# Moving the second block's sums, one weight conversion and one expert's matrix in an attention, experts and dense kernel

## The chip, the cores and the metric

The kernel runs on one core of a Trainium2 chip. The metric is the device time in microseconds of one execution. An execution is one launch of one program, which holds all three parts of the computation.

A core has five engines that each run their own list of instructions in order and wait for one another by semaphores: TensorE (PE; matrix products, its weight loads shown as PEld), VectorE (DVE), ScalarE (ACT), GpSimd (POOL) and SyncE (SP). Transfers are issued by SyncE and GpSimd here. "Issue" of a transfer and its landing are told apart below.

## The reference, cut to what matters

Three functions are chained. 4 x 8 heads, 1152 positions and a head dimension of 64 give 2304 tokens of 512 after attention.

```python
def attention(q, k, v):
    q_pool = q.reshape(B, H, S // 2, 2, D).mean(axis=3)
    a = softmax(q_pool @ k.T / sqrt(D))
    return a @ v                          # 2304 tokens x 512 in the end

def experts(x, w_skip, w_gate, w1, w2):
    do = x @ w_skip > 0                   # the others pass unchanged
    e = argmax(x[do] @ w_gate); gate = its softmax
    for e in range(8):                    # w1[e] 512x1024, w2[e] 1024x512
        y[mask_e] = gate * (relu(x[mask_e] @ w1[e]) @ w2[e])
    x[do] += y

def dense(x, w_in, w_out):                # w_in 512x2048, w_out 2048x512, both float64
    h = x @ w_in
    return ((h - tanh(h)) @ w_out).astype(float32)
```

The two matrices of the last part come in as float64, 8 MB each. The kernel reads them as pairs of 32-bit words and makes a high and a low part of each on the chip ("conversion" below).

## The kernel before

**Order.** The program is written under a manual schedule: each engine runs its instructions in the order in which the Python code writes them down. So the place of a line in the code is its place in the queue of its engine, and an instruction that waits holds back all that stands behind it on that engine. Attention and the router come first, then `Experts`, then `Dense`.

**Wide: the float64 matrices.** `Wide` cuts both matrices into 16 jobs of 1 MB of raw words, 8 of `w_in` (results in `wi`) and then 8 of `w_out` (results in `wo`). `load(i)` sends job i from SyncE's queue into one of two raw buffers, `raw[i % 2]`. The conversion of a job is three VectorE operations on 128x1024 words (`steps`, lines 769 to 773, into the tile `wa`), then a ScalarE copy for the high part (line 783) and one VectorE operation for the low part (line 784 or 785). `queue` makes a list of small steps of several jobs: the ScalarE copy and the low part of one job are woven into the first steps of the next, and the load of job i + 2 is sent with the third step of job i. So a list of n jobs has 4n pieces, the last of which holds the last copy and low part.

**Experts.** The tokens are sorted by expert on the chip, experts by falling count of tokens, in tiles of 128. How many there are is known only on the chip, so tiles stand in nested conditions that every engine takes with its own branch (`place`, `chain`, `tile`; lines 952, 973 and 977). A tile (`tile(a, j)`: expert a, tile j) gathers its tokens, multiplies by the first matrix (line 917, `ps_bh`), by the second (line 917 too, `ps_by`), and stores the result to DRAM (`ys`) in the next tile. `load(a, i)` sends the first (i = 0, buffers `f1`) or second (i = 1, buffers `f2`) matrix of expert a from GpSimd's queue, in two halves of 1 MB, behind a condition on the count of tokens; the count `n` and the expert's number `e` are read into registers of GpSimd with the first matrix. `split1` and `split2` turn pieces of the matrices into a high and a low float16 part (`c1`, `c2`; named `w1s`, `w2s` in the trace) with one ScalarE and one VectorE operation each, line 877 and the line behind it. The first matrix of expert a + 1 is sent in the first tile of expert a, once the last `split1` of a is written down; its second matrix later in the same tile. Three `split1` pieces of the next expert stand at the end of an expert's last tile, behind a condition. `SIDE` says how many jobs of `Wide` are converted in which tile (11 in all; `Dense.LATE` must hold the rest), and the loads for the next tile's jobs stand at the end of each tile.

**The way to the dense stage.** `Experts.run` stores the last tile from GpSimd; `before` sends the gather for block 0 of the dense stage from GpSimd; `after` (`Dense.first`) takes the very last tile's rows from SBUF by a product with a selection matrix.

**Dense.** The 2304 tokens are 9 blocks of 256. `fetch(n)` loads a block's rows from SyncE (`fetch_x`) and gathers the experts' results by two gathers on GpSimd (`fetch_y`, tile `cy`, line 1054). `mix(n, a)` adds gate times expert result to half a block on VectorE (line 1064). `transp(n, a)` makes a high part on ScalarE (line 1092) and a low part on VectorE (line 1093), and sends two transposing transfers from SyncE (line 1096) into `xT`; block 0 is transposed on TensorE instead. A step `(n, u)` is an eighth of the hidden dimension for a block: `hid` makes 24 matrix products (lines 1108 to 1110), three ScalarE operations, five VectorE operations (lines 1119 to 1123), a ScalarE copy (1124) and a subtraction on GpSimd (1125). `proj` takes the results of the step two before and makes 12 products with `w_out` (lines 1141 to 1143). The first 16 steps go over blocks 0 and 1 in the order four steps of block 0, four of block 1, then alternating; steps 16 to 71 take blocks 2 to 8 one after the other. So step 4 is the first that needs block 1.

Beside the steps, `run` takes one piece of the list of late conversions in each step (two in steps listed in `TWICE`), and by `side` the sums and transposes of blocks 1 and 2: halves of block 1 behind steps 1 and 2, of block 2 behind steps 9 and 11. `setup` sends the first two raw loads of the late jobs before anything else of this stage, and `fetch(1)` stands in `run`.

Of the kernel before, what the change touches and what calls it, by code (L numbers as in the profile page):

```python
# [9 lines left out]
F32 = mybir.dt.float32  # L10
# [470 lines left out]
E = 8  # L481
# [328 lines left out]
class Experts:  # L810
# [6 lines left out]
    SX, S1, S2 = 2.0 ** 8, 2.0 ** 4, 2.0 ** 8  # L817
    SIDE = {(0, 1): 2, (0, 2): 2, (0, 3): 2, (0, 4): 1, (1, 1): 2, (1, 2): 1, (1, 3): 1}

# [33 lines left out]
    def load(self, a, i, half=(0, 1)):  # L853

        if a == E:
            return
        nc, pool = self.nc, (mybir.EngineType.Pool,)
        if i == 0 and 0 in half:
            self.n, self.e = self.reg(self.perm[:, 0], a, self.MOST[a], pool), self.reg(self.perm[:, 1], a, E - 1, pool)
        with self.tc.If(self.n > 0) if a else ExitStack():  # L860
            src = (self.w1, self.w2)[i][ds(self.e, 1)].rearrange("o (k p) f -> p (o k) f", p=P)
            for k in half:
                nc.gpsimd.dma_start(out=(self.f1, self.f2)[i][k],
                                    in_=src[:, 4 * k:4 * k + 4] if i else src[:, :, 512 * k:512 * k + 512])
# [14 lines left out]

    def split1(self, f):  # L880
        w = slice(f * P, (f + 1) * P)
        v = slice(f % 4 * P, (f % 4 + 1) * P)
        self.split([t[:, :, w] for t in self.c1], self.f1[f // 4][:, :, v], self.S1)

# [22 lines left out]
    def tile(self, a, j, base, n):  # L907
# [11 lines left out]
        if j == 0:  # L919
            for f in range(self.PRE, 8):  # L920
                self.split1(f)
            self.load(a + 1, 0)
        aside(3)
# [27 lines left out]
        if a + 1 < E:  # L951
            with self.tc.If(self.end <= j + 1):
                for f in range(self.PRE):
                    self.split1(f)
        aside(len(side))
        if a + j:
            for i in self.groups.get((a, j + 1), ())[:2]:
                self.wide.load(i)

    def place(self, a):  # L960
# [20 lines left out]
    def run(self, before, after):  # L981
        nc = self.nc
        self.fetch(0)
        self.load(0, 0, (1,))
        self.load(0, 1)
        last = self.reg(self.more[:, 0], 0, CAP - 1, (mybir.EngineType.Pool,))
        nc.scalar.activation(self.py.rearrange("p (a t) -> p a t", a=4),
                             self.ident32.unsqueeze(1).to_broadcast([P, 4, P]), AF.Copy, scale=0.0)
        T = mybir.EngineType
        T = (T.Activation, T.Pool, T.DVE, T.SP)  # L990
        self.tiles = self.count(0)
        for f in range(2):
            self.split1(f)
        self.transp()
        for f in range(2, self.PRE):
            self.split1(f)
        self.fetch(1)
        few = self.reg(self.more[:, 0], 1, 1, T)
        self.place(0)
        self.tc.mark_branch_hint_location("few", hint=few, engines=T)  # L1000
        before()
        self.evac()
        self.store(last)
        after()
        with self.tc.If(few > 0, label="few"):
            some = [self.reg(self.perm[:, 0], a, self.MOST[a], T) for a in range(2)]
            for (a, j), jobs in self.groups.items():
                with self.tc.If(some[a] <= j):
                    for i in jobs:
                        self.wide.load(i)  # L1010
                        self.wide.run([i])


class Dense:


    T2 = 0.04
    LATE = 5
    TWICE = (5, 6, 7, 8)
    ORDER = (0, 8, 1, 2, 3, 4, 5, 6, 7)  # L1020
# [7 lines left out]

    def setup(self, ctx, wide):
        tc, self.wide = self.tc, wide  # L1030
        jobs = range(len(wide.jobs) - self.LATE, len(wide.jobs))
        for i in jobs[:2]:
            wide.load(i)
        self.late = wide.queue(jobs, jobs[2:])
        pool = lambda n, b: ctx.enter_context(tc.tile_pool(name=n, bufs=b))
        self.wp = pool("c_w", 1)
        self.io, self.xt, self.tm, self.gp = pool("c_io", 2), pool("c_xt", 2), pool("c_tm", 2), pool("c_g", 4)
        ps = lambda n, b: ctx.enter_context(tc.tile_pool(name=n, bufs=b, space=PSUM))
        self.ps_h, self.ps_o = ps("ps_ch", 4), ps("ps_co", 4)

# [120 lines left out]
    def run(self):  # L1161
# [7 lines left out]
        NB = NT // 2  # L1169
        self.fetch(1)  # L1170
        for a in range(2):
            self.transp(0, a)
        halves = [(n, u) for u0 in (0, 4) for n in range(2) for u in range(u0, u0 + 4)]
        steps = halves[:8] + sorted(halves[8:], key=lambda s: (s[1], s[0])) + [(n, u) for n in range(2, NB) for u in range(8)]
        side = {1: (1, 0), 2: (1, 1), 9: (2, 0), 11: (2, 1)}
        for s, (n, u) in enumerate(steps):
# [3 lines left out]
            for _ in range(2 if s in self.TWICE else 1):  # L1180
                if self.late:
                    self.late.pop(0)()
            if s in side:
                self.mix(*side[s])
                self.transp(*side[s])
            if n > 1 and u in (2, 4):
# [15 lines left out]
def pooled_attention__moe__tanhshrink_kernel(ctx, tc, q, k, v, moe_w_skip, moe_w_gate, moe_w1, moe_w2,  # L1202
                                             moe2_w_in, moe2_w_out, out):
    nc = tc.nc
# [6 lines left out]
    with tc.manual_schedule():  # L1211
# [59 lines left out]
        with ExitStack() as cctx:  # L1271
            dense.setup(cctx, Wide(cctx, tc, moe2_w_in, moe2_w_out, wi, wo))
            dense.run()
# [30 lines left out]
```

## Time and profile before

| | us |
|---|---|
| Median of three runs | 1036.32 |
| Lowest and highest of them | 1034.73, 1036.73 |
| The profiled execution, its own time | 1031.25 |
| Span of the profiled execution | 1029.8 |
| TensorE busy in it | 937.1 (91%) |
| VectorE busy | 780.3 (76%) |
| ScalarE busy | 633.4 (62%) |
| GpSimd busy | 517.3 (50%) |

TensorE's granted clock is 0.966 of full speed in the mean. The time of a profiled execution and its span differ by what lies before the first and after the last instruction; both are of one execution, and the profiled one lies below the median of the runs. A share of busy time is a mean over three stages that have different limits, so the table says little of what a change in one stage does; the page's strip of 40 slices and the timelines do.

### The profile page before, as it was taken

Reading aid. Unit: us, or ns where it says so; the run is one execution under the profiler, and the core shown is the slowest. Engines: PE = TensorE matmul, PEld = TensorE weight load, DVE = VectorE, ACT = ScalarE, POOL = GpSimd, SP = SyncE. Lnnn points to the kernel's source line nnn. Section 1 sums busy time; section 2 is a strip of 40 time slices with the busy share of each in tenths; the row PEclk is TensorE's granted clock in tenths of the full one; section 3 lists DMA queues with packets and bytes.
Section 4 is the critical chain, followed back from the end, with each engine's and each line's share of the span. In section 5 each row is a group of like instructions: output and inputs, shape, how many; then the busy total and the mean of one; then the engine's idle time right before and its main releaser. Section 6 shows DMA issues by size and latency. Waiting matters only on the chain. (4 is left out here: it accounts for less than half of the span.)

```text
span 1029.8 us, 25570 instructions
## 1 busy us (share of the span) xinstructions
PE 937.1 (91%) x10249; PEld 700.1 (68%) x10249; DVE 780.3 (76%) x1436; ACT 633.4 (62%) x1203; POOL 517.3 (50%) x476
## 2 busy tenths in 40 slices
PE   5689999999999999949999676998999999999998
PEld 2356666666666666637776544876888888888886
DVE  8689889888888998768887547788566566666654
ACT  4588999888999998835353534444445444454443
POOL 7958998888899986533132221323222322322221
PEclk9899999999999999978999888999999999999999
DMA  7776978666785730059774535221221211112100
GB/s 222 152 162 192 207 186 214 135 127 109 168 160 129 156 72 15 28 197 348 231 242 163 191 90 162 71 52 44 60 52 40 64 42 52 52 34 70 21 22 20
DMA packets 129728, 122.43 MB, mean 119 GB/s; under 512 B 92270, under 2 KB 96878, under 8 KB 128558
## 3 DMA queue, kind: packets, MB, share of 16 engines
q1 hardware_dynamic: 121790, 92.48, 36.1%
q0 software_dynamic: 7792, 28.05, 8.2%
q8 instruction: 86, 1.41, 0.6%
q14 instruction: 60, 0.49, 0.2%
HBM read 74.73 MB, written 19.14 MB: 91 GB/s over the span
## 5 line engine op out<-in xcount | busy, mean ns | idle before, releaser
L242 POOL TENSOR_TENSOR pl<-p,ph 128x512 f16<-128x512 f32 x214 | 264.6, 1256 | 55.4 <-ACT p L237 41.5
L188 DVE TENSOR_REDUCE m<-ps_m 128x1 f32<-128x384 f32 x432 | 225.2, 546 | 35.2 <-PE ps_m L187 32.9
L1125 POOL TENSOR_TENSOR gl<-v,gh 128x512 fp32r<-128x512 f32 x71 | 93.6, 1319 | 290.0 <-ACT gh L1124 286.6
L236 ACT ACTIVATE ph<-ps_e 128x512 f16<-128x512 f32 x279 | 176.9, 634 | 53.9 <-PE ps_e L248 50.7
L1108 PE MATMUL ps_ch<-xT,wi 128*128 128x256 f16 x576 | 159.7, 277 | 10.0 <-DMA xT<-xs 9.3
L299 PEld LDWEIGHTS <-ph 128*128 128x128 f16 x2304 | 132.6, 99 | 49.5 <-issue 22.3
L1124 ACT CAST gh<-v 128x512 fp32r<-128x512 f32 x72 | 44.5, 618 | 189.4 <-DVE v L1123 189.4
L1109 PE MATMUL ps_ch<-xT,wi 128*128 128x256 f16 x576 | 158.9, 276 | 0.4 <-DVE xT L1093 0.4
L1110 PE MATMUL ps_ch<-xT,wi 128*128 128x256 f16 x576 | 158.9, 276 | 0.0
L187 PE MATMUL ps_m<-ks,qT 128*128 128x384 f16 (+1 forms) x480 | 121.6, 334 | 23.7 <-DVE m L188 16.3
L299 PE MATMUL ps_a<-vh,pl 128*128 128x65 f16 x1152 | 135.9, 195 | 0.0
L299 PE MATMUL ps_a<-vh,ph 128*128 128x65 f16 x1152 | 135.9, 195 | 0.0
L299 PE MATMUL ps_a<-vl,ph 128*128 128x65 f16 x1152 | 135.7, 194 | 0.0
L237 ACT ACTIVATE p<-ps_e 128x512 f32<-128x512 f32 x211 | 134.5, 637 | 0.0
L1119 DVE SCALAR_TENSOR_TENSOR v<-u,ps_ch 128x512 f32<-128x512 f32 x72 | 49.3, 685 | 111.7 <-ACT t L1117 109.0
L1141 PE MATMUL ps_co<-wo,gh 128*128 128x512 f32 x288 | 120.4, 418 | 3.1 <-ACT wo L783 3.1
L1143 PE MATMUL ps_co<-wo,gl 128*128 128x512 f32 x288 | 114.6, 398 | 0.7 <-POOL gl L1125 0.7
L1142 PE MATMUL ps_co<-wo,gh 128*128 128x512 f32 x288 | 114.2, 397 | 1.0 <-DVE wo L785 1.0
L247 PE MATMUL ps_e<-qT,ks 128*128 128x512 f16 x288 | 110.8, 385 | 2.6 <-DVE pl L242 1.8
L248 PE MATMUL ps_e<-qT,kh 65*128 65x512 f16 x288 | 111.3, 386 | 1.9 <-DMA qT<-mt 1.9
L299 PEld LDWEIGHTS <-pl 128*128 128x128 f16 x1152 | 107.9, 98 | 0.0
L187 PEld LDWEIGHTS <-qT 128*128 128x128 f16 (+1 forms) x480 | 42.7, 101 | 66.0 <-issue 31.3
(222 smaller groups left out, 2084.7 us busy)
## 6 DMA issues: line engine op xcount, KB each, us to landing
v<-in_v_dram SPq DMA_DIRECT2D x16, 576.0 KB
k<-in_k_dram SPq DMA_DIRECT2D x15, 576.0 KB
q<-in_q_dram SPq DMA_DIRECT2D x16, 512.0 KB
raw<-in_moe_w_in_dram SPq DMA_DIRECT2D x8, 1024.0 KB
w1f<-in_moe_w_dram POOLq DMA_DIRECT2D x8, 1024.0 KB, 6.9
w2f<-in_moe_w_dram POOLq DMA_DIRECT2D x8, 1024.0 KB, 9.6
raw<-in_moe_w_out_dram SPq DMA_DIRECT2D x8, 1024.0 KB
ys<-zero SPq DMA_DIRECT2D x5, 1280.0 KB
```

The lines of the kernel that those rows point to most:

```text
L187: nc.tensor.matmul(ps[o, 0:384], w, ks[:, h, c * 384:(c + 1) * 384], start=True, stop=True)
L188: nc.vector.tensor_reduce(out=s["m2"][:, i, c:c + 1], in_=ps[:, 0:384], axis=AX.X, op=ALU.max)
L236: nc.scalar.activation(ph, ps, AF.Exp, scale=2.0 ** -20)
L237: nc.scalar.activation(src, ps, AF.Exp, scale=2.0 ** -20)
L242: (nc.vector if dve else nc.gpsimd).tensor_tensor(out=pl, in0=src, in1=ph, op=ALU.subtract)
L299: self.nc.tensor.matmul(o, x, r, start=first and i == 0, stop=k == NKT - 1 and i == 2, skip_group_check=True)
L1108: nc.tensor.matmul(ps[:, a], self.wi[0][:, w], xh[:, c], start=c == 0, stop=False)
L1109: nc.tensor.matmul(ps[:, a], self.wi[0][:, w], xl[:, c], start=False, stop=False)
L1110: nc.tensor.matmul(ps[:, a], self.wi[1][:, w], xh[:, c], start=False, stop=c == 3)
L1141: nc.tensor.matmul(o, gh[:, a, s], self.wo[0][:, w], start=f == 0, stop=False)
L1142: nc.tensor.matmul(o, gh[:, a, s], self.wo[1][:, w], start=False, stop=False)
L1143: nc.tensor.matmul(o, gl[:, a, s], self.wo[0][:, w], start=False, stop=f == 15)
```

## The change

Three parts, with the lines that carry each.

- **Dense stage.** `side` becomes `{0: ((1, 0), (1, 1)), ...}`: both sums of block 1, then both halves' copies, subtractions and transposes, behind step 0 instead of one half each behind steps 1 and 2. `LATE` is 4 instead of 5 and `TWICE` is (0, 3) instead of (5, 6, 7, 8). `setup` is cut in two: the first sends `fetch(1)`, and `start` behind it the first two raw loads.
- **Experts, conversions.** `SIDE[(1, 2)]` is 2 instead of 1, so that 12 of the 16 jobs are converted beside the experts.
- **Experts, matrices.** The first matrix of expert a + 1 is sent in the first tile of a only for a < 2. For 0 < a < 6 the first matrix of expert a + 2 is sent at the end of the last tile of a, behind a new condition, from GpSimd's queue. For that the first matrices of experts 3, 5 and 7 lie in the two raw buffers of `Wide` (`first`). Where the second matrix is sent for a > 2, the count and the expert's number are read into registers again.

```diff
-    SIDE = {(0, 1): 2, (0, 2): 2, (0, 3): 2, (0, 4): 1, (1, 1): 2, (1, 2): 1, (1, 3): 1}
+    SIDE = {(0, 1): 2, (0, 2): 2, (0, 3): 2, (0, 4): 1, (1, 1): 2, (1, 2): 2, (1, 3): 1}
...
-        if i == 0 and 0 in half:
+        if i == 0 and 0 in half or i and a > 2:
             self.n, self.e = self.reg(self.perm[:, 0], a, ...), self.reg(self.perm[:, 1], a, ...)
         with self.tc.If(self.n > 0) if a else ExitStack():
...
-                nc.gpsimd.dma_start(out=(self.f1, self.f2)[i][k],
+                nc.gpsimd.dma_start(out=(self.first(a), self.f2)[i][k],
...
+    def first(self, a):
+        if a < 3 or a % 2 == 0:
+            return self.f1
+        return [t.rearrange("p (o f) t -> p o (f t)", o=4).bitcast(F32) for t in self.wide.raw]
+
-    def split1(self, f):
+    def split1(self, a, f):
...
         if j == 0:
             for f in range(self.PRE, 8):
-                self.split1(f)
-            self.load(a + 1, 0)
+                self.split1(a, f)
+            if a < 2:
+                self.load(a + 1, 0)
...
         if a + j:
             for i in self.groups.get((a, j + 1), ())[:2]:
                 self.wide.load(i)
+        if 0 < a < E - 2:
+            with self.tc.If(self.end <= j + 1):
+                self.load(a + 2, 0)
...
-    LATE = 5
-    TWICE = (5, 6, 7, 8)
+    LATE = 4
+    TWICE = (0, 3)
...
-    def setup(self, ctx, wide):
+    def setup(self, ctx):
...
+        self.fetch(1)
+
+    def start(self, wide):
         jobs = range(len(wide.jobs) - self.LATE, len(wide.jobs))
         for i in jobs[:2]:
             wide.load(i)
...
-        self.fetch(1)
         for a in range(2):
             self.transp(0, a)
...
-        side = {1: (1, 0), 2: (1, 1), 9: (2, 0), 11: (2, 1)}
+        side = {0: ((1, 0), (1, 1)), 9: ((2, 0),), 11: ((2, 1),)}
...
-            if s in side:
-                self.mix(*side[s])
-                self.transp(*side[s])
+            for f in (self.mix, self.transp):
+                for x in side.get(s, ()):
+                    f(*x)
...
-            dense.setup(cctx, Wide(cctx, tc, moe2_w_in, moe2_w_out, wi, wo))
+            dense.setup(cctx)
+            dense.start(Wide(cctx, tc, moe2_w_in, moe2_w_out, wi, wo))
             dense.run()
```

## Rows read from the trace of the kernel before

**Rows 1.** Table by stretches: stretch, us, busy us of each engine (instructions), clock, DMA.
```profile
core 0: us, PE busy (x) PEld busy (x) DVE busy (x) ACT busy (x) POOL busy (x), PEclk, DMA share, GB/s
650.00:713.00 63.00, 62.67 (x420) 50.83 (x417) 53.89 (x75) 28.55 (x49) 18.24 (x13) 1.00 0.23 59
...
717.80:721.20 3.40, 3.40 (x10) 2.62 (x9) 3.20 (x6) 0.62 (x1) 1.35 (x2) 0.50 0.55 120
```
**Rows 2.** TensorE's timeline, dense stage: start, us, line, operation, [idle before, releaser].
```profile
625.16 0.50 PE L1143 MATMUL ps_co<-wo,gl 128*128 128x512 f32 x1 [0.53 <-POOL gl L1125]
...
627.61 0.28 PE L1108 MATMUL ps_ch<-xT,wi 128*128 128x256 f16 x1
...
642.50 0.37 PE L1108 MATMUL ps_ch<-xT,wi 128*128 128x256 f16 x1 [9.31 <-DMA xT<-xs]
...
649.74 0.28 PE L1108 MATMUL ps_ch<-xT,wi 128*128 128x256 f16 x1
...
710.06 0.28 PE L1108 MATMUL ps_ch<-xT,wi 128*128 128x256 f16 x1
...
715.95 0.50 PE L1141 MATMUL ps_co<-wo,gh 128*128 128x512 f32 x1 [3.10 <-ACT wo L783]
...
721.63 0.28 PE L1108 MATMUL ps_ch<-xT,wi 128*128 128x256 f16 x1
```
**Rows 3.** TensorE's timeline, third expert's tile and fourth's: first-matrix matmuls.
```profile
568.91 5.52 PE L917 MATMUL ps_bh<-bxt,w1s 128*128 128x128 f16 x96 [1.07 <-PEq L973]
...
587.78 7.28 PE L917 MATMUL ps_bh<-bxt,w1s 128*128 128x128 f16 x96 [7.73 <-ACT w1s L877]
```
**Rows 4.** The page's list of DMA issues: count, KB each, us to landing.
```profile
w1f<-in_moe_w_dram POOLq DMA_DIRECT2D x8, 1024.0 KB, 6.9
```
**Rows 5.** VectorE's timeline, dense stage, steps 0 to 2 and a later sum.
```profile
620.06 0.69 DVE L1119 SCALAR_TENSOR_TENSOR v<-u,ps_ch 128x512 f32<-128x512 f32 x1 [6.27 <-ACT t L1117]
...
622.95 0.68 DVE L769 TENSOR_SCALAR wa<-raw 128x1024 uint32<-128x1024 uint32 x1
...
627.66 1.21 DVE L771 SCALAR_TENSOR_TENSOR wa<-raw,wa 128x1024 uint32<-128x1024 uint32 x1
628.79 1.75 DVE L1064 SCALAR_TENSOR_TENSOR cx<-cy,gate,cx 128x512 f32<-128x512 f32 x1
...
694.15 0.74 DVE L1064 SCALAR_TENSOR_TENSOR cx<-cy,gate,cx 128x512 f32<-128x512 f32 x1
```
**Rows 6.** The chain that ended last, just before TensorE's wait at 642.50 ends.
```profile
638.07 0.63 ACT xs L1092
...
638.72 3.65 DMA xT<-xs
```
**Rows 7.** SyncE's timeline: issue times of transposes and of a raw slice.
```profile
631.24 2.59 SPq L1096 DMA_TRANSPOSE xT<-xs  x2
...
636.39 0.38 SPq L762 DMA_DIRECT2D raw<-in_moe_w_out_dram  x1
```
**Rows 8.** GpSimd's timeline, step 1's subtraction.
```profile
628.50 1.50 POOL L1125 TENSOR_TENSOR gl<-v,gh 128x512 fp32r<-128x512 f32 x1 [3.39 <-ACT gh L1124]
```
**Rows 9.** View of tile cy, 614 to 617 us: the gathers for the second block.
```profile
DMA to landing us min/median/max: 8.7/8.7/8.7
```
**Rows 10.** TensorE's branches at the tiles' ends: count: min/median/max ns, starts.
```profile
L973 PEldq COMPARE_BRANCH  x2: 189/271/353, 564.2 to 568.0; - x2
...
L973 PEldq COMPARE_BRANCH  x1: 7422/7422/7422, 579.5 to 579.5; - x1
...
L977 PEldq COMPARE_BRANCH  x2: 185/1948/3710, 599.9 to 604.0; - x2
...
L952 PEldq COMPARE_BRANCH  x2: 72/134/197, 563.8 to 563.9; - x2
```
**Rows 11.** ScalarE's waits, 564 to 570 us: us, count, longest.
```profile
ACT w1s L877 <- issue: 4.2, 1, 4.2
```
**Rows 12.** GpSimd's register loads and semaphore adjustments, 589 to 598 us.
```profile
L846 POOLq TENSOR_LOAD <-perm x4: 287/290/291, 591.2 to 594.6; - x4
...
L860 POOLq INC_SWDGE_SEM  x2: 928/942/957, 592.8 to 596.4; - x2
```

More of the change, by code (lines that the diff above doesn't have):

```diff
@@ L878, in split @@
         self.nc.vector.scalar_tensor_tensor(out=lo, in0=src, scalar=s, in1=hi, op0=ALU.mult, op1=ALU.subtract)
-    def split1(self, f):
+    def first(self, a):
[3 more added lines that the diff above has]
+    def split1(self, a, f):
         w = slice(f * P, (f + 1) * P)
         v = slice(f % 4 * P, (f % 4 + 1) * P)
-        self.split([t[:, :, w] for t in self.c1], self.f1[f // 4][:, :, v], self.S1)
+        self.split([t[:, :, w] for t in self.c1], self.first(a)[f // 4][:, :, v], self.S1)
     def split2(self, f):
@@ L953, in tile @@
                 for f in range(self.PRE):
-                    self.split1(f)
+                    self.split1(a + 1, f)
         aside(len(side))
@@ L992, in run @@
         for f in range(2):
-            self.split1(f)
+            self.split1(0, f)
         self.transp()
         for f in range(2, self.PRE):
-            self.split1(f)
+            self.split1(0, f)
         self.fetch(1)
@@ L1027, in __init__ @@
         self.X[0] = [pool.tile([P, 2, DM], F32, name="c%s0" % n) for n in "xy"]
-    def setup(self, ctx, wide):
-        tc, self.wide = self.tc, wide
+    def setup(self, ctx):
+        pool = lambda n, b: ctx.enter_context(self.tc.tile_pool(name=n, bufs=b))
+        self.wp = pool("c_w", 1)
+        self.io, self.xt, self.tm, self.gp = pool("c_io", 2), pool("c_xt", 2), pool("c_tm", 2), pool("c_g", 4)
+        ps = lambda n, b: ctx.enter_context(self.tc.tile_pool(name=n, bufs=b, space=PSUM))
+        self.ps_h, self.ps_o = ps("ps_ch", 4), ps("ps_co", 4)
+        self.fetch(1)
+    def start(self, wide):
         jobs = range(len(wide.jobs) - self.LATE, len(wide.jobs))
@@ L1034, in setup @@
         self.late = wide.queue(jobs, jobs[2:])
[L1035 to L1039, printed above, removed]
     def fetch(self, n):
```

## The prediction

> **What bounds the kernel now.** I read the page first, for the stages: attention to 440 us, routing, the experts to 601, a handover, and the dense stage from 613 to the end. The diff touches nothing before the experts, so the question is who ends the waits from 465 us on. The table by stretches answers it for most of the dense stage: from 650 to 713 us TensorE is busy 62.67 of 63 us [rows 1], so nothing that only relieves another engine gains there. What can be gained is where TensorE stands still, and its own timeline, read by the brackets, has three such places from 568 us on. At 642.50 it waited 9.31 us for the transposed second block, and at 715.95 it waited 3.10 us for the last converted slice of the output matrix [rows 2]; at 587.78, between the third expert's only tile and the fourth's, it waited 7.73 us [rows 3]. All three are touched. The page's list of transfers shows that the first matrix is fetched in 8 halves, so only four experts have tokens here [rows 4]: the new place for later experts' matrices matters for the fourth expert alone.
>
> **Part 1, the second block's sums, and the dense stage's conversions.** Today VectorE does step 0's five operations from 620.06 to 622.95, then one conversion step, then step 1's five, another conversion step, and only then the first sum at 628.79; the other sum waits behind step 2's [rows 5]. From the second half's ScalarE copy (0.63 us) to the landing of its transpose goes 3.65 us [rows 6], stretched because SyncE had sent a 1 MB load of raw weights at 636.39, ahead of that pair [rows 7]. TensorE gets its block at 642.50.
>
> After the change, both conversion steps and both sums follow step 0. Worked out on VectorE: 622.95 plus 0.68 and 1.21 [rows 5] is 624.8. The first sum then meets GpSimd's subtraction for step 0, which stands behind a cast of step 0's last result, by my estimate from 623.9 to 625.4. In before the same meeting stretched the sum to 1.75 us, ending half a microsecond after GpSimd's subtraction of 1.50 us (628.50 to 630.00) [rows 5, 8]; so I end it at 625.9. The second sum, unhindered 0.74 [rows 5], ends at 626.6. Two copies of 0.63 on ScalarE and two subtractions as long on VectorE end at 627.9 [rows 6]. SyncE needs 2.59 us for a pair of transposes [rows 7]; four of them from 626.5 are issued by 631.7 and land by 632.9, since the load of the next raw slice now stands behind them.
>
> So the transposes no longer end the wait; what is late next is step 1, pushed back on VectorE by the sums. Its two ScalarE reads follow the copies, its five VectorE operations run 628.3 to 631.3 (2.9 to 3.0 us, as for step 0), the cast ends at 632.0, GpSimd's subtraction at 633.4. From the arrival of that operand a projection lasts 2.45 us (625.16 to 627.61) [rows 2]. TensorE is through with step 1's projection at 635.8 and starts step 4. A step at full speed lasts 5.48 us (710.06 less 649.74, the starts of steps 16 and 5, over 11) [rows 2], so step 5 starts at 641.3 instead of 649.74: **8.5 us**, of which 6.7 is waiting and 1.8 a clock that had fallen during the long wait. If the shorter gaps (some 1.6 and 1.4 us) also drop it, 6.7 is left.
>
> The wait at 715.95: with five conversions in this stage the last one is taken up at step 15, when TensorE already wants it. Four conversions make 16 pieces; two are taken at steps 0 and 3, so the last is done at step 13. By my running sum (five operations of 3.0 and one piece of some 1.2 per step of 5.48, and the block 2 sums at steps 9 and 11) VectorE reaches it near 696, and TensorE needs it near 704. The whole wait goes. It cost more than its bracket: from step 16's start to the next one's (710.06 to 721.63) it took 11.57 us instead of 5.48 [rows 2], because TensorE ran at half clock afterwards, granted 0.50 from 717.8 to 721.2 [rows 1]. **6.1 us**; 3.1, the bracket alone, is the lower end.
>
> The fetch of block 1 is sent before the raw slices instead of behind them. It is not the last thing that the sums wait for; the gather on GpSimd is (8.7 us to landing [rows 9]), and it still follows the last expert's store. 0 here, up to 0.5 lost if the earlier transfer slows the handover's gathers.
>
> **Part 2, the fifth conversion goes to the second expert's third tile.** Four VectorE operations of 0.68 to about 1.2 us [rows 5], 4.3 us together, in a tile whose matmuls take some 11 us (5.52 for the first matrix [rows 3], about as long for the second). Two conversions and the tile's own three operations fill 10.7 of these 11, so it mostly hides, but the next tile's conversion starts late and stands before an operation that TensorE wants: between 0 and 1.5 us, I take 0.75.
>
> **Part 3, the fourth expert's first matrix.** The 2 MB leave the third expert's tile and are sent at the end of the second expert's last tile. What they meet are branches. At 579.5 TensorE's branch took 7422 ns, at the end of the last expert (nothing large in flight) the same kind took 3710, at the end of the second expert 353 and 189 [rows 10]. The slow one starts while a first matrix and half of a second are in flight. I read 3.71 as fetching code and the rest as waiting behind 2 MB; without the first matrix I expect 4 to 5.2, a gain of 2.2 to 3.4, and I take **3.0**. The bounds are 0 and 5.5 (all 3.7, and the 1.76 by which 7.28 exceeds 5.52 at a low clock [rows 3]).
>
> The Trainium skill ("DMA: Bandwidth & Descriptors", section on queues, rings and completion order) says that a DMA engine takes turns between its queues packet by packet. By that rule a code fetch on its own queue would not stand behind megabytes, the extra 3.7 us would have another cause, and the gain here would be 0, the total 3 us smaller. The rows (7422 against 3710) do not decide the cause, which is why 0 is the bound.
>
> What is given back: ScalarE waited 4.2 us after its own branch at the second expert's end [rows 11], and now the 2 MB are in flight there. Its conversions feed the next tile. Bounds: 0.4, if it only shifts with part 2, and 3.5, if its fetch is held as TensorE's was; I take **1.5**. GpSimd gets two more register loads (0.29 each) for each second matrix, and at each tile's end a condition. Not taken, it costs one semaphore adjustment of 0.94 us [rows 12]. In the tiles before the last these hide behind GpSimd's waits for matmuls. At the fourth expert's end they don't: GpSimd goes straight on to the gather that opens the dense stage, and every later gather, the store and the raw loads queue behind that. Two loads, an adjustment and two branches: 0.7 to 2.2, I take **1.9**.
>
> **Sum.** -8.5 - 6.1 + 0.75 - 3.0 + 1.5 + 1.9 = -13.45 us. The profiled execution took 1031.25 (span 1029.8), which makes 1017.8 there; it lies 5.07 below the median of the runs, 1036.32. Against the median: **1022.9 us**.
>
> **Rivals.**
> (a) Block 1 is late all the same. VectorE works in order, so if the gather lands later than 624.8, every operation of step 1 waits behind the first sum. Landing 3 us later takes 3 us and the 1.8 of clock: -13.45 + 4.8 = -8.65, 1027.7 us. For it: 8.7 us to landing, behind two 1 MB loads [rows 9]. Against: 0.5 MB fewer now share that stretch.
> (b) The code-fetch wait moves rather than shrinks: TensorE's branch at the second expert's end takes 7.42 instead of 0.35 because the moved matrix is in flight, with 1.76 us of low clock, and the one at 579.5 stays as it is. Instead of -3.0 and +1.5: +7.1 + 1.76. Total -3.1, 1033.2 us. Against: TensorE's branch stands at 564.2, before the new transfer can flow.
> (c) Slower: the new condition at the tile ends costs TensorE a code fetch each time, 3.71 us in each of the six tiles of experts two to four: 22.3 us, total +8.8, 1045.1 us. It decides from four tiles (14.8 us). Against: the condition that already stands at a tile's end took 72 to 197 ns [rows 10]. The Trainium skill ("Runtime: NRT & Kernel Launch", instruction fetch mechanics) says that a taken branch whose target is outside the two code pages at hand stalls for a fetch. By that rule it hangs on how the added code shifts the pages; no row of before shows where they lie.
> (d) The change does not do what it says: the raw buffers stay in use, the fourth expert's matrix lands no earlier, and the dense stage alone gains: -14.6 + 0.75 + 1.9 = -11.95, 1024.4 us, inside the forecast's own range.
>
> **How the numbers follow.** Forecast with (d) 0.68, (a) 0.15, (b) 0.10, (c) 0.07. The forecast's own range, from its bounds: best -8.5 - 6.1 - 5.5 + 0.4 + 0.7 = -19.0, 1017.3 us; worst -6.7 - 3.1 + 1.5 + 3.5 + 2.2 + 0.5 = -2.1, 1034.2 us. Not all bounds fall together; leaving out some 2 in 10 on the upper side and with (a) inside, I give 1017 to 1031. A difference under 0.2% (2.1 us) can't be told from none: below 1034.2 is faster. The forecast and (a) are faster nearly whole, (b) half: 0.86 faster, 0.07 same, 0.07 slower.
>
> **What would show it.** In TensorE's timeline the wait of 9.31 us should be gone, with two short ones of 1 to 2 us for GpSimd's and ScalarE's operands of step 1 in its place. No wait for the output matrix's conversion after step 13, and no 0.50 clock there. TensorE's branch after the third expert's tile should take 4 to 5.2 us. The gather that opens the dense stage should come about 1.9 us later after the last expert's matmuls. I am wrong if step 4 waits for the transposes, if a branch of several microseconds appears at the second expert's end, or if VectorE ends the waits in steps 5 to 13.

## The result, and the profile after

The changed kernel took 1025.25 us (median of four runs), the kernel before 1035.53 beside it: 10.3 us less, a ratio of 0.9895, 95% interval 0.9872 to 0.9918. The forecast was 13.45 us less. The profiled execution took 1022.40 us, 8.85 less than that of before.

TensorE's timeline of the dense stage comes first: start, duration, line, operation, and in brackets how long TensorE stood idle before and what ended it. L1120 here is L1108 of before, L1153 to L1155 are L1141 to L1143.

```profile
618.43 0.37 PE L1120 MATMUL ps_ch<-xT,wi 128*128 128x256 f16 x1 [0.68 <-ACT xT L1104]
...
631.00 0.50 PE L1155 MATMUL ps_co<-wo,gl 128*128 128x512 f32 x1 [1.50 <-POOL gl L1137]
...
637.52 0.50 PE L1153 MATMUL ps_co<-wo,gh 128*128 128x512 f32 x1 [1.28 <-ACT gh L1136]
...
639.10 0.50 PE L1155 MATMUL ps_co<-wo,gl 128*128 128x512 f32 x1 [0.85 <-POOL gl L1137]
...
641.53 0.28 PE L1120 MATMUL ps_ch<-xT,wi 128*128 128x256 f16 x1
...
646.96 0.28 PE L1120 MATMUL ps_ch<-xT,wi 128*128 128x256 f16 x1
...
707.02 0.28 PE L1120 MATMUL ps_ch<-xT,wi 128*128 128x256 f16 x1
...
712.45 0.28 PE L1120 MATMUL ps_ch<-xT,wi 128*128 128x256 f16 x1
```

Of before three more rows of this timeline are needed, the third tile's transposes and second matrix, and the stage's first matmul:

```profile
574.27 0.60 PE L892 MATMUL ps_bt<-ident,bx 128*128 128x128 f32 x4
574.71 5.34 PE L917 MATMUL ps_by<-w2s,bhid 128*128 128x512 f16 x24
...
613.12 0.37 PE L1108 MATMUL ps_ch<-xT,wi 128*128 128x256 f16 x1 [0.69 <-ACT xT L1092]
```

The 9.31 us before step 4 [rows 2] are gone. In their place stand three short stops: 1.50 us for GpSimd's subtraction of step 0, whose stop in before was 0.53 [rows 2], then 1.28 and 0.85 for ScalarE's and GpSimd's operands of step 1. The first comes of GpSimd's subtraction taking 2.22 us (its timeline), while VectorE has a conversion step and the first sum beside it; in before it took 1.28 us (from 623.84):

```profile
628.72 2.22 POOL L1137 TENSOR_TENSOR gl<-v,gh 128x512 fp32r<-128x512 f32 x1 [6.69 <-ACT gh L1136]
```

Step 5 starts at 646.96, 28.53 us behind the stage's first matmul, where in before it was 36.62 (613.12 to 649.74): 8.1 us gained. From step 16's start to step 17's (707.02 to 712.45) it takes 5.43 us where it took 11.57 [rows 2]: 6.1 us gained. From the first matmul to the end of the span the stage takes 402.35 us instead of 416.65.

But the stage now begins at 618.43 instead of 613.12. Here 5.3 of those 14.3 us are lost, and the experts' part of TensorE's timeline shows where about half of them go (third expert's tile and the start of the fourth's; L923 is L917 of before):

```profile
570.78 5.52 PE L923 MATMUL ps_bh<-bxt,w1s 128*128 128x128 f16 x96 [1.08 <-ACT w1s L877]
...
578.83 1.08 PE L898 MATMUL ps_bt<-ident,bx 128*128 128x128 f32 x4 [2.52 <-DMA bx<-xd,bix]
579.97 6.60 PE L923 MATMUL ps_by<-w2s,bhid 128*128 128x512 f16 x24
...
592.24 7.25 PE L923 MATMUL ps_bh<-bxt,w1s 128*128 128x128 f16 x96 [5.67 <-ACT w1s L877]
```

The wait before the fourth tile has shrunk from 7.73 [rows 3] to 5.67 us. But there is a new stop of 2.52 us in the middle of the third tile, and behind it 24 matmuls take 6.60 us at a fallen clock, as the table by stretches shows (stretch, us, busy us of PE, PEld, DVE, ACT, POOL, mean granted clock, DMA share, GB/s):

```profile
578.50:586.50 8.00, 7.47 (x28) 3.25 (x28) 6.55 (x11) 7.27 (x14) 3.64 (x5) 0.79 0.33 81
```

So from the third tile's start to the fourth's it takes 21.46 us (570.78 to 592.24) instead of 18.87 (568.91 to 587.78): 2.6 us longer, where the forecast had it 3.0 shorter.

The bracket names the gather of the tokens. That gather was sent at 565.32, ahead of the 2 MB, and had landed long before (5.6 us by the list of transfers). ScalarE stopped in the same place and went on in the same moment, for a store that was sent still earlier. Its timeline, and GpSimd's:

```profile
578.81 0.60 ACT L902 ACTIVATE by<-ps_by 128x512 f32<-128x512 f32 x1 [4.50 <-DMA ys<-by]
```

```profile
565.32 1.94 POOL L872 DMA_INDIRECT bx<-xd,bix  x1 [1.24 <-PE ps_bt L898]
567.68 1.55 POOL L863 DMA_DIRECT2D raw<-in_moe_w_dram  x2 [0.42 <-DVE bxt L878]
```

Two engines that go on in the same moment point to a third. The view of line 983, the nested condition, between 564 and 580 us has it (queue, operation, count, shortest, median and longest in ns, first and last start; POOLq is GpSimd's own list of waits and branches, and PEldq further below is TensorE's); and below it the same view of before, between 562 and 571 us, where that line is 973:

```profile
L983 POOLq EVENT_SEMAPHORE  x6: 17/30/6861, 569.3 to 571.0; - x6
...
L983 POOLq INC_SWDGE_SEM  x1: 873/873/873, 577.9 to 577.9; - x1
```

```profile
L973 POOLq EVENT_SEMAPHORE  x5: 17/43/4407, 564.2 to 564.5; - x5
L973 POOLq INC_SWDGE_SEM  x1: 807/807/807, 569.0 to 569.0; - x1
```

At the end of the second expert GpSimd comes to the join of the nested conditions. There it waits for the transfers that it has in flight (EVENT_SEMAPHORE, the longest 6.86 us), and then adjusts their semaphores (INC_SWDGE_SEM). In before the last of them was the token gather, and the adjustment ended at about 569.8. Now the fourth expert's 2 MB stand in front of the join. They land at about 577.8 (the second half is issued at 568.5 and takes 9.3 us to land), and the adjustment ends at 577.9 + 0.87 = 578.7. TensorE and ScalarE go on at 578.83 and 578.81.

### The profile page after: what moved, and what is told of

Same layout as the page of the kernel before. It is cut to its first block, busy times and chain, and to the rows that moved or that the text cites. A ratio compares the mean times of both kernels' runs of the same rounds, so it can differ in the third digit from the quotient of the medians.

```text
span 1020.8 us, 25654 instructions
## 1 busy us (share of the span) xinstructions
PE 934.6 (92%) x10249; PEld 698.3 (68%) x10249; DVE 777.7 (76%) x1436; ACT 631.7 (62%) x1203; POOL 518.2 (51%) x476
## 3 DMA queue, kind: packets, MB, share of 16 engines
q8 instruction: 87, 1.43, 0.6%
## 5 line engine op out<-in xcount | busy, mean ns | idle before, releaser
L1120 PE MATMUL ps_ch<-xT,wi 128*128 128x256 f16 x576 | 158.7, 275 | 0.7 <-ACT xT L1104 0.7
L1153 PE MATMUL ps_co<-wo,gh 128*128 128x512 f32 x288 | 119.7, 416 | 1.3 <-ACT gh L1136 1.3
L1155 PE MATMUL ps_co<-wo,gl 128*128 128x512 f32 x288 | 113.9, 396 | 2.4 <-POOL gl L1137 2.3
```

Source lines behind the costliest of these rows:

```text
L1120: nc.tensor.matmul(ps[:, a], self.wi[0][:, w], xh[:, c], start=c == 0, stop=False)
L1153: nc.tensor.matmul(o, gh[:, a, s], self.wo[0][:, w], start=f == 0, stop=False)
L1155: nc.tensor.matmul(o, gl[:, a, s], self.wo[0][:, w], start=False, stop=f == 15)
```

## The experiments

Two theories of the new stop were put to the chip. **J**, the join: GpSimd passes the join only when the 2 MB have landed, and its adjustment is what the two engines wait for. **C**, the code: the engines' own instructions come late, behind 2 MB of bulk. The forecast's theory, that the new place costs next to nothing, was the third. The times of the places that matter, all worked out from the starts in TensorE's timelines and the views of its branches (us; the last column from the stage's first matmul to the end of the span):

| kernel | third tile to fourth | stop before its transposes | branch behind it | fourth tile to dense | dense stage |
|---|---|---|---|---|---|
| before | 18.87 | none | 7.42 | 25.34 | 416.65 |
| changed | 21.46 | 2.52 | 5.04 | 26.19 | 402.35 |
| changed, again | 20.67 | 1.47 | 5.22 | 26.74 | 402.77 |
| part 3 alone | 22.58 | 3.08 | 5.61 | 26.95 | 416.81 |
| part 3 undone | 18.28 | none | 6.81 | 27.12 | 403.90 |
| behind the join | 18.37 | none | 6.90 | 26.40 | 402.47 |
| behind the join, again | 17.78 | none | 6.27 | 26.36 | 402.76 |
| sums alone | 18.28 | none | 6.74 | 26.32 | 411.05 |
| conversions alone | 17.75 | none | 6.28 | 26.34 | 409.79 |
| rows behind raw | 20.61 | 1.43 | 5.22 | 26.58 | 403.71 |

### Part 3 undone

```diff
-            if a < 2:
-                self.load(a + 1, 0)
+            self.load(a + 1, 0)
...
-        if 0 < a < E - 2:
-            with self.tc.If(self.end <= j + 1):
-                self.load(a + 2, 0)
```

> The changed kernel with part 3 undone: every first matrix is sent in the first tile of the expert before it, into its own buffers, with no condition at the tile's end. Theory J (GpSimd's join at the second expert's end waits for the 2 MB that now stand before it, and its semaphore adjustment is what ScalarE's eviction and TensorE's transposes in the third expert's tile wait for): the stop of 2.52 us in that tile and its half clock go, the stop of about 7.7 before the fourth tile comes back, so from the third tile's start to the fourth's 18.9 us as in before instead of 21.46, and from there to the dense stage 25.3 instead of 26.2: 3.4 us faster than the changed kernel, 1021.8 us. The forecast's theory (part 3 costs 0.4 net: -3.0 + 1.5 + 1.9): 1024.9.

Measured: 1022.51 us, 0.9882 (0.9866 to 0.9899) of before. The stop is gone and the longer branch is back, as J has it. The time does not part the theories: 1022.51 lies nearer to J's 1021.8 than to the forecast's 1024.9, but against the kernel before beside each, the gain over the changed kernel is only 1.3 us (0.9882 against 0.9895), and the interval holds both. The way from the fourth tile to the dense stage did not get shorter (27.12), so that part of the expectation fails: what the condition costs there can't be told from how much that stretch varies.

### Part 3 alone

The kernel before with part 3 of the diff, and nothing else of it.

> Part 3 alone on the kernel before: sums, conversions and their count as they were. Theory J: the third tile 2.6 us longer and the way to the dense stage 0.85, nothing given back later, since the dense stage is bound by what starts with it: 3.4 us slower than before, 1038.9 us. The forecast's theory: 0.4 slower, 1035.9.

Measured: 1039.01 us, 1.0038 (1.0023 to 1.0053) of before: 4.0 us slower, clear of noise. The forecast's 0.4 falls. TensorE's timeline and the view of line 983:

```profile
580.04 0.63 PE L898 MATMUL ps_bt<-ident,bx 128*128 128x128 f32 x4 [3.08 <-DMA bx<-xd,bix]
```

```profile
L983 POOLq EVENT_SEMAPHORE  x1: 8711/8711/8711, 570.3 to 570.3; - x1
L983 POOLq INC_SWDGE_SEM  x1: 873/873/873, 579.1 to 579.1; - x1
```

Again TensorE goes on 0.1 us behind the end of the adjustment (579.1 + 0.87).

### The matrix sent behind the join

```diff
         if j == 0:
+            if a >= 2:
+                self.load(a + 1, 0)
             for f in range(self.PRE, 8):
                 self.split1(a, f)
...
-        if 0 < a < E - 2:
-            with self.tc.If(self.end <= j + 1):
-                self.load(a + 2, 0)
```

> The changed kernel with the fourth expert's matrix still in the raw buffers, but sent at the top of the third expert's tile, behind the join, and no condition at the tile's end. Theory J: no stop at the transposes of the third tile, since the join waits for the token gather alone, as in before; the matrix is sent at about 571.5 instead of 572.4, so TensorE's branch at the tile's end stands behind nearly as much as in before: 6.5 to 7.4 us; 1021.3 us. Rival C (TensorE's and ScalarE's own code is what is late in the third tile, held up by 2 MB in flight): the 2 MB are in flight from 571.5 to some 579, and a stop of 1 to 2.5 us stays at the transposes: 1023 to 1024.5.

Measured: 1022.55 us, 0.9881 (0.986 to 0.9903). The raw buffers and the 2 MB are the changed kernel's; only the place in GpSimd's queue differs, and the stop is gone (timelines of TensorE, this run and its repetition):

```profile
577.02 0.60 PE L898 MATMUL ps_bt<-ident,bx 128*128 128x128 f32 x4
577.47 5.34 PE L923 MATMUL ps_by<-w2s,bhid 128*128 128x512 f16 x24
590.04 2.19 PE L923 MATMUL ps_bh<-bxt,w1s 128*128 128x128 f16 x19 [7.24 <-ACT w1s L877]
```

```profile
576.40 0.61 PE L898 MATMUL ps_bt<-ident,bx 128*128 128x128 f32 x4
576.84 5.34 PE L923 MATMUL ps_by<-w2s,bhid 128*128 128x512 f16 x24
```

> The kernel of the run behind the join once more, for a second trace and beside the others: third tile's start to the fourth's 18.3 to 18.9 us, no stop at its transposes, 1020 to 1023 us.

Measured: 1019.42 us, 0.9868 (0.9849 to 0.9887), with 1034.43 and 1032.30 of before beside the two runs. No stop in either trace, as J has it; the second one's 17.78 us from tile to tile and its time lie a little under what was expected. C wants a stop here, since the 2 MB, sent at 573.26, are in flight when TensorE comes to the transposes at 577.02, and there is none. But they were sent 1.6 us behind the start of that tile, and in the changed kernel 3.1 us ahead of it, so this run alone does not close C.

### The changed kernel again

> The changed kernel once more, beside the others of this call, for a second trace of it and a comparison on one chip: 1023 to 1026 us; theory J expects again a stop of 2 to 3 us before the transposes of the third expert's tile, right behind GpSimd's semaphore adjustment, and from that tile's start to the fourth's 21 to 22.6 us.

Measured: 1024.60 us, 0.9908 (0.9884 to 0.9932). The stop is there again, though shorter (1.47), and the third tile takes 20.67 us, a little less than expected. The kernels that keep the 2 MB off the join lie lower than this one (0.9868 to 0.9882 against 0.9895 and 0.9908), but the intervals touch: that they beat it is shown by the traces' third tile and the 4.0 us of part 3 alone rather than by these times.

### GpSimd held, with nothing in flight

To part the join from the bulk, GpSimd was kept from the join by memsets, and the matrix sent behind the join.

```diff
+        if 0 < a < E - 2:
+            with self.tc.If(self.end <= j + 1):
+                for _ in range(5):
+                    self.nc.gpsimd.memset(self.wide.raw[1].rearrange("p f t -> p (f t)").bitcast(F32), 0.0)
```

> The kernel of the run behind the join, with the condition at the tile's end back, but in it five GpSimd memsets of a raw buffer (by the 0.525 us of a 128x512 memset some 2.1 us each, 10.5 in all) in place of the 2 MB: GpSimd reaches the join about as late as in the changed kernel, and no large transfer is in flight. Theory J: TensorE stops before the transposes of the third expert's tile for 1.5 to 3 us and ScalarE before its eviction for about 4, both until just behind GpSimd's semaphore adjustment. Rival C (code held up by the bulk transfer): no stop there, since nothing but the token gather is in flight. Afterwards the matrix lands some 8 us later than in that run, so the time says little: 1026 to 1031 us.

Measured: 1029.30 us, one run. ScalarE's eviction waited 1.97 us, until 579.55, 0.1 us behind the end of GpSimd's adjustment (578.6 + 0.83), with no large transfer in flight; but the adjustment ended just as TensorE came to the transposes, so TensorE did not stop, against J's number. The hold was too short to decide TensorE's case.

```profile
579.55 0.60 ACT L902 ACTIVATE by<-ps_by 128x512 f32<-128x512 f32 x1 [1.97 <-DMA ys<-by]
```

> The hold again with seven memsets instead of five (1.8 us each by the first hold, whose adjustment ended just when TensorE came to the transposes, so that only ScalarE's eviction waited). GpSimd's adjustment now ends some 9 us behind the start of the third expert's tile. Theory J: TensorE stops before the transposes of that tile for 3 to 3.7 us and ScalarE before its eviction for 5 to 6, both ending within 0.2 us of the adjustment's end, with no large transfer in flight. Rival C: no stop there.

Measured: 1032.18 us, one run. TensorE's and ScalarE's rows, GpSimd's, the view of the join's line (986 here), and the DMA engines' busy share in 40 slices of 570 to 581 us:

```profile
580.86 1.09 PE L898 MATMUL ps_bt<-ident,bx 128*128 128x128 f32 x4 [5.32 <-DMA bx<-xd,bix]
```

```profile
580.79 0.60 ACT L902 ACTIVATE by<-ps_by 128x512 f32<-128x512 f32 x1 [7.25 <-DMA ys<-by]
```

```profile
566.38 13.00 POOL L971 MEMSET raw<- 128x2048 f32 x7
```

```profile
L986 POOLq INC_SWDGE_SEM  x1: 826/826/826, 579.8 to 579.8; - x1
```

```profile
DMA  0000000000020000000000000000000000000000
```

The DMA engines are as good as empty, and TensorE still stops, for 5.32 us, ScalarE for 7.25, and both go on 0.1 to 0.2 us behind the adjustment's end at 580.7. The stops are longer than forecast because the memsets began only 3.6 us ahead of the tile's first matmul (566.38 to 570.02), not 5.2 as in the hold of five; where they end is what was to be decided. C falls and J holds. The brackets still say "DMA bx" and "DMA ys", though neither was in flight.

### The branch without the second matrix

```diff
-        if j == 0:
+        if j == 0 and a != 2:
             self.load(a + 1, 1)
```

> The kernel of the run behind the join without the load of the fourth expert's second matrix (left out: its tokens are multiplied by the third expert's), so nothing large is in flight when TensorE branches at the end of the third expert's tile. If that branch is a code fetch of some 3.7 us and the rest waiting behind bulk, it takes 3.5 to 4.2 and the wait before the fourth tile is 4.0 to 4.6 us instead of 7.24. If it is a price of this branch whatever is in flight, 7 us again. Time 1018 to 1020 us by the first, 1022.5 by the second.

Measured: 1015.96 us, one run. The view of TensorE's branch at the third expert's end, with the 2 MB of the second matrix in flight (the run behind the join) and without:

```profile
L982 PEldq COMPARE_BRANCH  x1: 6901/6901/6901, 582.3 to 582.3; - x1
```

```profile
L982 PEldq COMPARE_BRANCH  x1: 3429/3429/3429, 584.0 to 584.0; - x1
```

The branch halves, the wait before the fourth tile is 3.75 us instead of 7.24, and from the third tile's start to the fourth's it takes 14.89 us. So half of this wait stands behind bulk. The Trainium skill ("DMA: Bandwidth & Descriptors", section on queues, rings and completion order) has an engine take turns between its queues packet by packet; read as "a code fetch does not stand behind megabytes", that does not describe these two rows, and the measurement decides.

### Sums alone

The kernel before with this edit only:

```diff
-        side = {1: (1, 0), 2: (1, 1), 9: (2, 0), 11: (2, 1)}
+        side = {0: ((1, 0), (1, 1)), 9: ((2, 0),), 11: ((2, 1),)}
```

> The kernel before with block 1's sums and transposes behind step 0, and nothing else changed (five conversions, twice at steps 5 to 8, block 1's rows sent behind the raw slices). The forecast's first term: the wait of 9.31 us goes, step 5 comes 8.1 to 8.5 us earlier, the stop of 3.1 us at step 16 with its half clock stays: 1027.1 to 1027.5. The rival (a) (the gather lands behind two raw slices and the sums hold step 1 back on VectorE): 3 us and a fallen clock less gain, 1031.9. If the order of the block's rows and of the raw slices matters, this run shows it: with the rows behind, a stop of over 2 us before step 4.

Measured: 1029.04 us, 0.995 (0.9933 to 0.9968), beside 1034.43 for before: 5.4 us less, where some 8 were expected. Step 5 started 29.73 us behind the first step, 6.9 us earlier than in before and not 8.1 to 8.5, and in step 5 TensorE stopped for a converted slice (timelines of TensorE and VectorE):

```profile
653.23 0.50 PE L1142 MATMUL ps_co<-wo,gh 128*128 128x512 f32 x1 [1.78 <-DVE wo L785]
```

```profile
630.89 1.42 DVE L1064 SCALAR_TENSOR_TENSOR cx<-cy,gate,cx 128x512 f32<-128x512 f32 x2 [1.68 <-DMA cx<-xd]
```

So two things were missed. The sums waited 1.68 us for block 1's rows, which stand behind two raw slices on SyncE. And with five conversions in the stage VectorE, which has taken the sums first, is late with a slice in step 5, so that part of the gain was given back. The stage took 411.05 us, 5.6 less than in before.

### Rows behind the raw slices

```diff
         self.ps_h, self.ps_o = ps("ps_ch", 4), ps("ps_co", 4)
-        self.fetch(1)
...
+        self.fetch(1)
         for a in range(2):
             self.transp(0, a)
```

> The changed kernel with block 1's rows and gathers sent behind the two raw slices, as in before. The forecast put this order at 0, up to 0.5 us: 1025.0 to 1025.8. The rival, from the run with the sums alone, where step 5 came 29.7 us behind the first step instead of 28.5: the rows land later and the sums wait for them, 1.2 us: 1026.4.

Measured: 1024.82 us, beside 1024.60 for the changed kernel: no difference that these runs can show. The trace shows one, in VectorE's timeline (this run, then the changed kernel):

```profile
632.48 1.41 DVE L1075 SCALAR_TENSOR_TENSOR cx<-cy,gate,cx 128x512 f32<-128x512 f32 x2 [1.15 <-DMA cx<-xd]
```

```profile
629.74 2.41 DVE L1076 SCALAR_TENSOR_TENSOR cx<-cy,gate,cx 128x512 f32<-128x512 f32 x2
```

The wait is 1.15 us and the dense stage 403.71 us, 1.1 above the mean of the changed kernel's two traces. But the run with part 3 undone, which has the rows ahead, took 403.90, so the stage varies by as much for other reasons. What the order is worth in time stays open; that it takes away a wait of 1.2 to 1.7 us in front of the sums is shown.

### Conversions alone

The kernel before with the new `SIDE`, `LATE` and `TWICE`.

> The kernel before with four conversions in the dense stage instead of five, two pieces at steps 0 and 3, and the fifth in the second expert's third tile; sums, order and matrices as before. The forecast's terms: -6.1 for the stop at step 16 and its half clock, +0.75 in the experts: 5.3 us faster, 1028.8 us; the wait of 9.3 us before step 4 stays. Rival: the earlier pieces push the second block's sums further back on VectorE, and the wait before step 4 grows by 1 to 2.5 us: 1030 to 1031.5.

Measured: 1027.11 us, 0.9936 (0.9916 to 0.9956), beside 1032.30 for before: 5.2 us less by the medians and 6.6 by the ratio, where 5.3 was expected. The stop at step 16 is gone, and the wait before step 4 did not grow but shrank, from 9.31 to 7.27 us (TensorE's timeline):

```profile
644.32 0.37 PE L1108 MATMUL ps_ch<-xT,wi 128*128 128x256 f16 x1 [7.27 <-DMA xT<-xs]
```

The rival falls. Why the wait shrank, no run shows. The stage took 409.79 us, 6.9 less. With the 5.6 of the sums alone that is 12.5. Both together gave 14.3 and 13.9 in the changed kernel's two traces, 14.2 and 13.9 behind the join, 12.9 with the rows behind the raw slices and 12.8 with part 3 undone, so this difference is no clear sign that the two help each other. What does show it is the stop of 1.78 us in step 5 for a slice that the fifth conversion makes: it stands in the run with the sums alone, and in no trace that has both.

### The second matrix early

To use both readings, the raw buffers took the fourth expert's second matrix, sent under a condition at the top of the second expert's last tile, and that tile converted nothing.

```diff
-    SIDE = {(0, 1): 2, (0, 2): 2, (0, 3): 2, (0, 4): 1, (1, 1): 2, (1, 2): 2, (1, 3): 1}
+    SIDE = {(0, 1): 2, (0, 2): 2, (0, 3): 2, (0, 4): 2, (1, 1): 2, (1, 2): 2}
...
+        if j:
+            self.ahead(a, j)
...
+    def ahead(self, a, j):
+        if 0 < a < E - 2:
+            with self.tc.If(self.end <= j + 1):
+                self.load(a + 2, 1)
```

> A version built on both readings: the raw buffers take the fourth expert's second matrix instead of its first, sent at the top of the second expert's last tile (long landed when GpSimd comes to the join), the first matrix goes as in before, and the last tile of the second expert converts nothing (one more conversion in the first expert's fifth tile). If the join is the price of part 3 and TensorE's branch stands behind bulk, there is no stop at the third tile's transposes and the branch at its end takes 3.4 to 4.2 us instead of 5.0 to 5.6: third tile's start to the fourth's 15 to 16 us, 1018 to 1020 us. If the branch's price has to do with the first matrix as well, which still lands shortly before, 5 us and more there, 1021 to 1022.5.

Measured: 1033.81 us, 1.0 of before (0.9985 to 1.0016). At the third tile it does what was expected: no stop, a branch of 4.19 us, and 15.64 us from that tile's start to the fourth's. But the second expert's tiles lost much more. The view of the raw loads' line on SyncE, of the condition's line on GpSimd, and VectorE's timeline:

```profile
L762 SPq EVENT_SEMAPHORE  x8: 17/28/26119, 517.7 to 557.9; - x8
```

```profile
L973 POOLq INC_SWDGE_SEM  x2: 692/693/694, 543.4 to 544.9; - x2
```

```profile
554.25 0.69 DVE L769 TENSOR_SCALAR wa<-raw 128x1024 uint32<-128x1024 uint32 x1 [11.40 <-DMA raw<-in_moe_w_out_dram]
```

SyncE held its next raw load for 26.1 us and sent it at 544.04, just when GpSimd had passed the condition that might have filled the same buffer (543.4 + 0.69); the changed kernel sent that load at 517.61. Most of the 26.1 us passed before GpSimd came to the condition. VectorE then waited 11.40 us for the slice. It is J once more, on another engine: a transfer under a condition, even one that is not taken, is paid for by whoever waits for GpSimd to come past it.

## Why the prediction was right, and where it was not

The direction, the time (1022.9 against 1025.25, inside the range) and the dense stage were right. The part on the experts was not: its three terms for part 3 came to 0.4 us in all and measured 3.5. The time falls inside the range because the dense stage's two terms are far larger. By the steps of the sum:

- **Block 1's sums, -8.5.** 8.1 measured. Step 4 no longer waits for the transposes, and two short stops for step 1's operands came, 1.28 and 0.85 us where 1 to 2 was forecast; the third, for step 0's subtraction, was not named. Two conditions of the term were not seen: with the fifth conversion still there it gave only 5.6, part of it lost to that conversion's slice and part to the rows; and the order of rows and raw slices, put at 0 because the gather would land last, covers a wait of 1.2 to 1.7 us for the rows.
- **The last conversion's wait, -6.1.** 6.1 measured, the bracket and the half clock behind it together; the lower bound of 3.1 would have been wrong.
- **The fifth conversion in the second expert's third tile, +0.75.** From the second expert's start to the third tile's, the four traces with twelve conversions and no matrix ahead of the join took 45.92 us in the mean (45.66 to 46.28), the two with eleven 45.18 and 45.17: 0.75.
- **The code fetch between the third tile and the fourth, -3.0.** Mis-sized. The branch takes 5.04 us in the changed kernel, inside the 4 to 5.2 forecast, but 7.42 was the longest that it took in any kernel: the mean of the six traces without the new place is 6.74, of the four with it 5.27. The gain is 1.5. The cause, waiting behind bulk, is shown by the branch of 3.43 us without the second matrix, and 4.19 where it was sent early.
- **ScalarE's code fetch, +1.5.** The failed step. The place was right, the second expert's end, and so was the cause, 2 MB that now stand there; the mechanism was another. The prediction knew GpSimd's semaphore adjustment and priced it at 0.94 us on GpSimd, then said that "in the tiles before the last these hide behind GpSimd's waits for matmuls". It did not ask what GpSimd waits for ahead of the adjustment, nor who waits for it. The join is now passed at 578.7 instead of 569.8; two engines stand, and the clock falls. ScalarE's own start is nearly unchanged: from the second expert's start to the third tile's the three traces with parts 2 and 3 took 46.02 us in the mean, against 45.92 with part 2 alone. The two parts do not simply add there: part 3 alone took 46.10, 0.9 above the 45.18 of neither, 0.6 of it in the second expert's first tile (11.60 us instead of 10.98).
- **The condition on the way to the dense stage, +1.9.** 26.62 us in the mean with it (four traces), 26.31 without (six, 25.34 to 27.12): 0.3, too little to tell from none. At the gather that opens the dense stage the price can be told: it is issued 4.84 to 5.14 us behind the end of the last expert's matmuls with the condition, 4.21 to 4.63 without, 0.5 us later in the mean and not 1.9. What takes up the rest was not shown.

From the third tile's start to the fourth's the new place costs 21.33 - 18.22 = 3.1 us in the mean. The sum as measured, with -14.1 for the dense stage (the mean of the changed kernel's two traces), is then -14.1 + 0.75 + 0.1 + 3.1 + 0.3 = -9.85, against -10.3 in the medians. The profiled execution of before was a quick one: from its first expert tile to the second expert's it took 60.34 us, the others 61.1 to 62.7, the two with the same code there included (the version with the second matrix early left out), so the two profiles are 1 to 2 us closer than the kernels are.

The rivals: (a) fell, the sums did not wait for the gather. (b) fell: TensorE's branch at the second expert's end took 348 ns at most. (c) fell: no branch of several microseconds came with the condition; what the traces show of it on TensorE is 0.2 to 0.6 us in the second expert's first tile. (d) fell, though its 1024.4 us lies nearest to the measured time: the matrix was sent earlier, 3.1 us ahead of the third tile's start and not 3.5 behind it, and landed earlier.

## What to carry to other kernels

Where a transfer stands under a run-time condition or ahead of a join, ask where the engine that issued it must wait for its landing before it goes on, and which engines wait for what it does next; the landing can then sit on their path even if the data are needed much later (here TensorE stood for 2.52 us ahead of a matrix that it used 13 us later). Send it behind the join, or early enough to have landed. When a bracket names a transfer that landed long ago, look for a semaphore adjustment that ended just before; and price two relieved waits together, since the engine that one relieves may be the one that the other needs.

## What the runs showed of the hardware

- GpSimd's semaphore adjustment behind a condition or a join takes 0.69 to 0.97 us, and other engines are held until its end, in six traces to within 0.3 us: TensorE for 5.32 us and ScalarE for 7.25 in the longer hold, with empty DMA engines, and SyncE for 26.1 us behind a condition that was not taken.
- TensorE's branch behind the third expert's tile took 3.43 us with nothing large in flight, 4.19 behind a first matrix sent 7 to 9 us before, 5.0 to 5.6 behind a second matrix, and 6.3 to 7.4 with a first and a second matrix sent in the 10 us before. The Trainium skill ("Runtime: NRT & Kernel Launch", instruction fetch mechanics) says that a taken branch whose target is outside the two code pages at hand stalls for a fetch; the rows agree in so far as this branch takes microseconds where others take 0.2 to 0.35 [rows 10], and add what bulk in flight does to it. Where the pages lie, no run shows.
- A stop of 2.52 us cost TensorE another 2.0 us behind it: from its transposes to the end of the tile's matmuls it took 7.74 us (578.83 to 586.57) instead of 5.78 in before (574.27 to 580.05), at a mean granted clock of 0.79 (578.5 to 586.5), a mixture of the two levels of 1.2 and 2.4 GHz.
